# The gate rows of a first-layer expert as a stream of their own, and gathers counted as landing later

## The chip, the cores and the metric

The kernel runs on one core of one Trainium2 chip. The metric is the device time of one execution in microseconds. TensorE (PE) multiplies and transposes, ScalarE (ACT), VectorE (DVE) and GpSimd (POOL) work element by element, SyncE (SP) issues the weight loads, and POOL also issues the indirect transfers (gathers and scatters of rows).

## The reference

What is computed, cut to its core: sparse attention with a linear distance bias, then a mixture-of-experts layer whose tokens pick an expert, then one whose experts take at most 384 tokens each in the order of the sorted gate logits.

```python
x = attention(q, k, v, n_global, n_local)          # 4*768 = 3072 tokens, 512 features
# layer 1: tokens with x @ w_skip > 0 only
e_idx = argmax(xc @ w_gate);  gate_w = softmax(xc @ w_gate)[e_idx]
for e in range(8):
    h = maximum(xc[mask] @ w1[e], 0);  y[mask] = gate_w[mask, None] * (h @ w2[e])
out[do_compute] = xc + y
# layer 2: cap = 3072 // 8 = 384
order = argsort(-(x @ w_gate).flatten())
for idx in order:                                  # greedy, until all are assigned
    tok, e = idx // 8, idx % 8
    if assigned[tok] < 0 and counts[e] < cap: assigned[tok] = e; counts[e] += 1
for e in range(8):
    out[mask] = maximum(x[mask] @ w1[e], 0) @ w2[e]
```

## The kernel before

Attention runs until about 227 us. Layer 1 follows until about 494 us: `run_units` walks over eight experts' units, each of up to 256 tokens (two blocks of 128) and eight slices `f` of the hidden width. A unit's tokens are gathered by number from `xd` (tile xg), transposed through the one PSUM bank pt into xh (high part) and xl (low part), and multiplied with the split weights wh and wl: twelve 256-column matmuls into ph a slice, then, one slice late (`finish`), six 512-column ones into py. ACT makes hh from ph, DVE makes hl. A weight chunk wr is split by `W_.pump`: ACT writes wh, then DVE or POOL writes wl.

Six units are plain. Then one "extra" unit `X_` takes the tokens that overflowed; its tokens' tile is xgx. The last two units hold their second products back (`defer`), and these run beside the routing of layer 2. Layer 2 (about 516 to 835 us) has eight units of 384 tokens, with one routing phase of the next expert between the matmuls of each.

When a unit's py is complete, `epi1` calls `rows2`: the output rows o0 and o1 are made on DVE and scattered to `x2d`. Layer 2's gate logits of these rows, called gate rows here, need five more steps: o0 is transposed through pt into x2t, o1 too, x2t is multiplied with wg into pr (8 small matmuls), ACT copies that to ls, two transposes follow, and DVE sums lgo, which POOL scatters to `l2d`. Before the change these steps are tasks, one popped at the end of each slice, whatever is ready then. `last_rows` is a routing task of a slice of unit 1: POOL numbers a tile (iota into a tile that shares its buffer with x2t), and DVE computes from it.

The order in which work of different streams stands between the matmuls is decided when the program is built. A clock `ck` estimates each engine's time; after each matmul `hook` lets the stream of the lowest rank go on whose inputs are estimated ready (`Stream.when`), and `wait_for` steps streams until a condition holds. For a gather the clock counts 2.7 us plus `ck.late` until it has landed.

```python
    def when(self):
        eng, aps = self.need
        if eng == "pt":
            return ck.ready("pe", last_pt, aps) + (T_LOW if lows else 0)
    ...
        end += 2.7 + (self.late if over else 0)
```

Of the kernel before, what the change touches and what calls it, by code (L numbers as in the profile page):

```python
# [161 lines left out]
def tile_attn_moe_moe(ctx: ExitStack, tc: tile.TileContext, q, k, v, n_global, n_local,  # L162
# [366 lines left out]
    ck.late = T_G  # L529
# [326 lines left out]
    class Unit:  # L856
        at, tb, py, defer, xh = None, 0, 0, None, None
# [280 lines left out]
    class Stream:  # L1138
# [12 lines left out]
        def when(self):  # L1151
            eng, aps = self.need
            if eng == "pt":
                return ck.ready("pe", last_pt, aps) + (T_LOW if lows else 0)
            t = ck.ready(eng, (), aps)
            return max(t, ck.at["dve"] - T_SP) if eng == "dve" else t
# [42 lines left out]
    RANK = {"x": X_B, "ids": 0.5, "main": 2, "extra": 4}  # L1199

    def start(kind, gen):
        s_ = Stream(gen)
        s_.kind = kind
        s_.rank = lambda: RANK[kind] if len(result) <= unit_no[0] + T_L else {"x": 0, "main": 1, "ids": 2, "extra": 4}[kind]
        streams.append(s_)
# [7 lines left out]
    def run_units(units, nb, epilogue, tasks=(), between=None):  # L1213
# [13 lines left out]
        for s in range(len(units) * FC):  # L1227
# [21 lines left out]
            if u + 1 < len(units):  # L1249
                V_ = units[u + 1]  # L1250
                if V_.at is None and (V_.is_ready() or f == FC - 1):
                    V_.ready()
                    if V_.at is None:
                        V_.load()
            W_.pump()
            W_.pump()
# [23 lines left out]
    def epi1(U_, tasks):  # L1280
        nb = len(U_.xs)
        if U_.defer is not None:
            if U_.defer == 0:
                tasks.append(lambda: gate2(U_))
# [4 lines left out]
            return  # L1289
        rows2(U_)  # L1290
        U_.x2t = fx_.tile([128, KC, 256], F32, name="x2t")

        def tr(tb):
# [4 lines left out]
            nc.scalar.activation(U_.x2t[:, :, tb * 128:(tb + 1) * 128], p, AF.Copy)  # L1298

        def lg():  # L1300
            p = fps.tile([128, 256], F32, name="pr")
            n = nb * 128
            for c in range(KC):
                nc.tensor.matmul(p[c * 32:(c + 1) * 32, :n], wg2[:, c, :], U_.x2t[:, c, :n], start=True, stop=True)
            U_.ls = fx_.tile([128, 256], F32, name="ls1")
            nc.scalar.activation(U_.ls[:, :n], p[:, :n], AF.Copy)

        def lt():
            p = fps.tile([128, HI, KC, 32], F32, name="pr")
            for tb in range(nb):  # L1310
                nc.tensor.transpose(p[:, tb].rearrange("p c e -> p (c e)"), U_.ls[:, tb * 128:(tb + 1) * 128], ident)
            lgo = ff.tile([128, HI, E], F32, name="lgo")
            nc.vector.tensor_reduce(lgo[:, :nb], p[:, :nb, :, :E].rearrange("p j c e -> p j e c"),
                                    axis=AX.X, op=OP.add)
            for tb in range(nb):
                scatter(l2d, U_.sid[:, tb:tb + 1], lgo[:, tb], l2_st)
            U_.tasks = None

        U_.tasks = tasks
        for tb in range(nb):  # L1320
            tasks.append(lambda tb=tb: tr(tb))
        tasks.append(lg)
        tasks.append(lt)
        if U_ is not X_:
            tasks.extend(rt_tasks[:3])
            del rt_tasks[:3]
# [73 lines left out]
    def last_rows(tb):  # L1400
        d = fx_.tile([128, 2, 128], F32, name="x2t")
# [79 lines left out]
    def extra_rest(hs_):  # L1481
# [23 lines left out]
        while units1[NE - 1].tasks:  # L1505
            units1[NE - 1].tasks.pop(0)()
        tasks = []
        epi1(X_, tasks)
        for ap, t in zip((X_.x2[0], X_.x2t, None), tasks):
            yield "pe", [ap if ap is not None else X_.ls]  # L1510
            t()

    def between(U_, finish):
        if U_.defer == 1:
            wait_for(lambda: not [s_ for s_ in streams if s_.kind == "extra"])
            fxx.close()
# [3 lines left out]
        return extra(U_, finish)  # L1520
# [271 lines left out]
    split_next()  # L1792
    units2[0].load()
    split_next()
# [40 lines left out]
```

## Time and profile before

| | |
|---|---|
| median of 3 runs | 835.23 us (834.9 to 835.77) |
| the profiled execution | 842.16 us, of which the span from first to last instruction is 840.2 us |
| mean granted TensorE clock | 0.958 of full speed |
| busy: PE | 767.8 us, 91% of the span |
| busy: DVE, POOL, ACT | 524.5 (62%), 423.3 (50%), 409.0 us (49%) |
| moved by DMA | 132.82 MB, 158 GB/s |

TensorE is busy for most of the span, and the other engines feed it. So one looks for the places where it is idle or slow. The profile gives times in microseconds from the span's start. A matmul's row shows its start, its length and, in brackets, the idle time of TensorE just before it with what ended it.

### The profile page before, as it was taken

To read this page: it belongs to the slowest core of one execution; us is meant where nothing else is said; L and a number is where in the kernel's file an instruction comes from. 1 tells how busy PE (TensorE), PEld (TensorE's weight loads), DVE (VectorE), ACT (ScalarE), POOL (GpSimd) and SP (SyncE) were. 2 spreads that over 40 slices of the span, in tenths; PEclk is the share of its full clock that TensorE was granted. 3 is DMA by queue.
4 is the path that set the end of the run, shared out by engine and by line. 5 is a ranking of instruction groups with operands and counts; after the bars stand their busy time and mean duration, and the time that the engine had idled before them with its cause. 6 is when DMAs were issued, how large, how long until landed. Compare 5 with 4: busy or idle time off the path is not lost.

```text
span 840.2 us, 16697 instructions
## 1 busy us (share of the span) xinstructions
PE 767.8 (91%) x5711; PEld 635.7 (76%) x5711; DVE 524.5 (62%) x1896; ACT 409.0 (49%) x923; POOL 423.3 (50%) x569
## 2 busy tenths in 40 slices
PE   7999998998889999998979957999999999899994
PEld 5887777776578777887768735788888888799993
DVE  6988979886556565554353576677787777822110
ACT  5887887875455455544452222343342534335311
POOL 4654566743224444533360524694765938568501
PEclk9999999999969999999999985999999999999997
DMA  7787898878146566356560043336263643555100
GB/s 178 185 207 190 227 226 230 229 203 234 45 150 215 184 218 231 135 178 204 166 230 6 17 135 125 132 115 195 99 225 113 190 142 135 177 175 169 39 31 37
DMA packets 141013, 132.82 MB, mean 158 GB/s; under 512 B 62523, under 2 KB 107835, under 8 KB 140928
## 3 DMA queue, kind: packets, MB, share of 16 engines
q1 hardware_dynamic: 132160, 111.09, 44.4%
q0 software_dynamic: 7168, 20.26, 7.0%
q8 instruction: 46, 0.75, 0.4%
q10 hardware_dynamic: 1600, 0.39, 0.2%
q14 instruction: 39, 0.32, 0.1%
HBM read 109.55 MB, written 23.49 MB: 158 GB/s over the span
## 4 chain that ended last, share of the span: by engine, by line
PE 33%; issue 19%; POOL 11%; DVE 3%; DMA 3%; ACT 1%; POOLq 0%; SPq 0%; DVEq 0%
PE ph L123 14%; PE py L123 14%; POOL wl L123 6%; PE pr L123 3%; PE pt L123 2%; POOL out_dram L123 2%; DMA wr<-in_moe_w_dram 2%; DMA xg<-xd,gid 1%; POOL xg L123 1%; DVE bank L123 1%; ACT wh L123 1%; POOL x2d L123 1%; POOL l2d L123 1%; DVE wl L123 0%; DVE gm L123 0%
## 5 line engine op out<-in xcount | busy, mean ns | idle before, releaser
L123 POOL TENSOR_TENSOR wl<-wr,wh 128x1024 fp32r<-128x1024 f32 (+1 forms) x97 | 205.0, 2133 | 114.4 <-ACT wh L123 113.9
L123 ACT ACTIVATE hh<-ph 128x384 fp32r<-128x384 f32 (+2 forms) x130 | 56.7, 436 | 214.4 <-PE ph L123 206.9
L123 ACT ACTIVATE wh<-wr 128x1024 fp32r<-128x1024 f32 (+1 forms) x148 | 140.7, 984 | 40.4 <-PE py L123 22.9
L123 DVE SCALAR_TENSOR_TENSOR hl<-ph,hh 128x256 fp32r<-128x256 f32 (+1 forms) x128 | 62.3, 487 | 123.7 <-ACT hh L123 114.5
L123 PE MATMUL py<-wh,hl 128*128 128x512 f32 x320 | 128.7, 402 | 2.1 <-DVE hl L123 2.1
L123 PE MATMUL py<-wh,hh 128*128 128x512 f32 x320 | 128.8, 403 | 0.0
L123 PE MATMUL py<-wl,hh 128*128 128x512 f32 x320 | 128.4, 401 | 0.0
L123 POOL TENSOR_SCALAR pb<-pb,st 128x232 f32<-128x232 f32 (+1 forms) x192 | 83.6, 454 | 72.7 <-ACT pb L123 26.9
L123 ACT ACTIVATE pb<-sb,st 128x232 f32<-128x232 f32 (+1 forms) x192 | 114.0, 664 | 10.2 <-DVE st L123 9.7
L123 PE MATMUL ph<-xh,wh 128*128 128x256 f32 (+1 forms) x512 | 106.4, 326 | 3.2 <-ACT wh L123 1.5
L123 PE MATMUL ph<-xh,wl 128*128 128x256 f32 (+1 forms) x512 | 104.4, 322 | 0.0
L123 PE MATMUL ph<-xl,wh 128*128 128x256 f32 (+1 forms) x512 | 103.0, 321 | 0.9 <-DVE xl L123 0.9
L123 PEld LDWEIGHTS ph<-xh,wh 128*128 128x128 f32 x512 | 84.7, 195 | 12.9 <-ACT wh L123 2.0
L123 PEld LDWEIGHTS ph<-xl,wh 128*128 128x128 f32 x512 | 82.9, 196 | 1.2 <-DVE xl L123 1.1
L123 PEld LDWEIGHTS ph<-xh,wl 128*128 128x128 f32 x512 | 83.2, 196 | 0.4 <-issue 0.2
L123 DVE TENSOR_TENSOR wl<-wr,wh 128x1024 fp32r<-128x1024 f32 x51 | 65.1, 1301 | 24.4 <-ACT wh L123 24.1
L123 PEld LDWEIGHTS py<-wh,hl 128*128 128x128 f32 x320 | 60.4, 189 | 14.9 <-DVE hl L123 3.2
L123 DVE CUSTOM_DVE_ANT_0 sb<-pS,bias 128x232 f32<-128x232 f32 (+1 forms) x192 | 61.5, 374 | 8.6 <-PE pS L123 7.0
L123 PEld LDWEIGHTS py<-wl,hh 128*128 128x128 f32 x320 | 60.6, 189 | 7.9 <-issue 0.3
L123 PEld LDWEIGHTS py<-wh,hh 128*128 128x128 f32 x320 | 60.9, 190 | 7.3
L123 DVE COPY pts<-pP 116x512 f32<-116x512 f32 (+1 forms) x96 | 60.7, 672 | 7.5 <-PE pP L123 7.1
L123 PE MATMUL pS<-kt,qt 64*128 64x232 f32 (+1 forms) x384 | 50.7, 382 | 1.0 <-ACT pb L123 1.0
(448 smaller groups left out, 1200.2 us busy)
## 6 DMA issues: line engine op xcount, KB each, us to landing
wr<-in_moe_w_dram SPq DMA_DIRECT2D x136, 512.0 KB
xd<-xs SPq DMA_DIRECT2D x32, 192.0 KB
x2d<-xs SPq DMA_DIRECT2D x32, 192.0 KB
kraw<-in_k_dram SPq DMA_DIRECT2D x30, 192.0 KB
qraw<-in_q_dram SPq DMA_DIRECT2D x30, 192.0 KB
vw<-in_v_dram SPq DMA_DIRECT2D x32, 160.0 KB
vw<-in_v_dram SPq DMA_DIRECT2D x32, 120.0 KB
xT<-in_moe_w_dram SPq DMA_DIRECT2D x1, 1536.0 KB
```

The lines of the kernel that those rows point to most:

```text
L123: r = f(*a, **k)
```

## The change

The gate rows become a generator `gate_rows`, started by `epi1` as a stream of the new kind "turn", with ranks between those of the others. `epi1` of the next unit and `last_rows` first wait until no such stream is left. The extra unit runs its own gate rows inside its stream, and no longer pops unit 5's tasks. `ck.late` goes from 1 to 2.0, except around the gathers of layer 2's first unit, where it is 0. A step that needs pt waits for `T_LOW` after DVE's estimated time, no longer after the rows' own. The second `W_.pump()` of a slice is left out in six plain units when the first did a split and one of the two chunks would be split by an engine other than POOL. The 16 gate products of unit 6 (`gate2`) move from a task of unit 7 to the point where unit 6 has finished, ahead of the last wait for the extra stream.

```diff
@@ -526,7 +526,7 @@
     WWT, WWN = 1, (2, 5)
     T_GAP, T_SP, T_EPS, T_W, T_P, T_L, T_F, X_B, T_H, T_M, LEAN, T_G, DIRECT, CUT = 0, 0.65, 0.1, 0, 8, 1, 0.3, 3, -4, 0, 2, 1, 13, 16
     T_LOW = 0.7
-    ck.late = T_G
+    ck.late = 2.0
     W_ = Weights()
 
     class Pacer:
@@ -854,7 +854,7 @@
     slot_rest = slot_ids(gid, sid, gwt, psl, tmp1)
 
     class Unit:
-        at, tb, py, defer, xh = None, 0, 0, None, None
+        at, tb, py, defer, xh, x2 = None, 0, 0, None, None, None
 
     def x_load(U_, nb):
         U_.xs, U_.xt, U_.at, U_.tb = [], {}, ck.at["pe"], 0
@@ -1151,7 +1151,8 @@
         def when(self):
             eng, aps = self.need
             if eng == "pt":
-                return ck.ready("pe", last_pt, aps) + (T_LOW if lows else 0)
+                t = ck.ready("pe", last_pt, aps)
+                return max(t, ck.at["dve"] + T_LOW) if lows else t
             t = ck.ready(eng, (), aps)
             return max(t, ck.at["dve"] - T_SP) if eng == "dve" else t
 
@@ -1196,12 +1197,12 @@
             flush()
             U_.tb += 1
 
-    RANK = {"x": X_B, "ids": 0.5, "main": 2, "extra": 4}
+    RANK = {"x": X_B, "turn": 3.5, "ids": 0.5, "main": 2, "extra": 4}
 
     def start(kind, gen):
         s_ = Stream(gen)
         s_.kind = kind
-        s_.rank = lambda: RANK[kind] if len(result) <= unit_no[0] + T_L else {"x": 0, "main": 1, "ids": 2, "extra": 4}[kind]
+        s_.rank = lambda: RANK[kind] if len(result) <= unit_no[0] + T_L else {"x": 0, "turn": 0.5, "main": 1, "ids": 2, "extra": 4}[kind]
         streams.append(s_)
 
     def split2(U_):
@@ -1252,8 +1253,11 @@
                     V_.ready()
                     if V_.at is None:
                         V_.load()
+            n = W_.split
             W_.pump()
-            W_.pump()
+            if (W_.split == n or W_.split == len(W_.order) or u >= NE or not W_.helped(W_.order[n])
+                    or not W_.helped(W_.order[W_.split])):
+                W_.pump()
             if tasks:
                 tasks.pop(0)()
         finish()
@@ -1281,49 +1285,46 @@
         nb = len(U_.xs)
         if U_.defer is not None:
             if U_.defer == 0:
-                tasks.append(lambda: gate2(U_))
                 tasks.append(lambda: gate2_rows(U_))
                 tasks.append(table)
                 tasks.extend([lambda: None] * 3)
                 tasks.append(table_clear)
             return
+        wait_for(turned)
         rows2(U_)
-        U_.x2t = fx_.tile([128, KC, 256], F32, name="x2t")
-
-        def tr(tb):
+        if U_ is not X_:
+            start("turn", gate_rows(U_, nb))
+            tasks.extend(rt_tasks[:3])
+            del rt_tasks[:3]
+
+    def turned():
+        return not [s_ for s_ in streams if s_.kind == "turn"]
+
+    def gate_rows(U_, nb):
+
+        n = nb * 128
+        x2t = fx_.tile([128, KC, 256], F32, name="x2t")
+        for tb in range(nb):
+            yield "pt", [U_.x2[tb]]
             flush()
             p = turns()
             for c in range(KC):
                 nc.tensor.transpose(p[:, c], U_.x2[tb][:, c * 128:(c + 1) * 128], ident)
-            nc.scalar.activation(U_.x2t[:, :, tb * 128:(tb + 1) * 128], p, AF.Copy)
-
...
-        U_.tasks = tasks
+            nc.scalar.activation(x2t[:, :, tb * 128:(tb + 1) * 128], p, AF.Copy)
+        yield "pe", [x2t[:, :, :n]]
+        p = fps.tile([128, 256], F32, name="pr")
+        for c in range(KC):
+            nc.tensor.matmul(p[c * 32:(c + 1) * 32, :n], wg2[:, c, :], x2t[:, c, :n], start=True, stop=True)
+        ls = fx_.tile([128, 256], F32, name="ls1")
+        nc.scalar.activation(ls[:, :n], p[:, :n], AF.Copy)
+        yield "pe", [ls[:, :n]]
+        p = fps.tile([128, HI, KC, 32], F32, name="pr")
         for tb in range(nb):
-            tasks.append(lambda tb=tb: tr(tb))
-        tasks.append(lg)
-        tasks.append(lt)
-        if U_ is not X_:
-            tasks.extend(rt_tasks[:3])
-            del rt_tasks[:3]
+            nc.tensor.transpose(p[:, tb].rearrange("p c e -> p (c e)"), ls[:, tb * 128:(tb + 1) * 128], ident)
+        lgo = ff.tile([128, HI, E], F32, name="lgo")
+        nc.vector.tensor_reduce(lgo[:, :nb], p[:, :nb, :, :E].rearrange("p j c e -> p j e c"), axis=AX.X, op=OP.add)
+        for tb in range(nb):
+            scatter(l2d, U_.sid[:, tb:tb + 1], lgo[:, tb], l2_st)
 
     BITS = ((27, 32), (22, 32), (17, 32), (12, 32), (7, 32), (2, 32), (0, 4))
     NH = CAP // 128
@@ -1398,6 +1399,7 @@
     keep = rt.tile([128, NT], F32, name="keep")
 
     def last_rows(tb):
+        wait_for(turned)
         d = fx_.tile([128, 2, 128], F32, name="x2t")
         tk = rt.tile([128, 2], F32, name="tk")
         nc.gpsimd.iota(d[:, 0], pattern=[[NT, 128]], base=0, channel_multiplier=0, allow_small_or_imprecise_dtypes=True)
@@ -1502,22 +1504,20 @@
                                  start=c == 0 and i == 0, stop=c == FC - 1 and i == 2)
             W_.free = 4 * NE + (c + 1) // 2
             W_.pump()
-        while units1[NE - 1].tasks:
-            units1[NE - 1].tasks.pop(0)()
-        tasks = []
-        epi1(X_, tasks)
-        for ap, t in zip((X_.x2[0], X_.x2t, None), tasks):
-            yield "pe", [ap if ap is not None else X_.ls]
-            t()
+        epi1(X_, [])
+        yield from gate_rows(X_, 1)
 
     def between(U_, finish):
         if U_.defer == 1:
+            finish()
+            wait_for(lambda: X_.x2 is not None)
+            gate2(units1[NE])
             wait_for(lambda: not [s_ for s_ in streams if s_.kind == "extra"])
             fxx.close()
         if U_.defer is not None:
             pool = f1x.enter_context(tc.tile_pool(name=f"h{U_.defer}", bufs=1)) if U_.defer else hp7
             U_.h = [pool.tile([128, FC, SLOTS], F32R, name=f"{n}{U_.defer}", bufs=1) for n in ("hh", "hl")]
-        return extra(U_, finish)
+        return extra(U_, finish) or U_.defer == 1
 
     for tb in range(HI):
         x_turn(units1[0], tb, f"py{tb}")
@@ -1790,7 +1790,9 @@
         need(W_.order[W_.split])
 
     split_next()
+    ck.late = 0
     units2[0].load()
+    ck.late = 2.0
     split_next()
     split_next()
     wait_for(lambda: units2[0].tb == NH)
```

Three places in TensorE's order, as the program lists it. The first is the end of unit 0, where unit 1 begins: o_4755 and o_4761 are unit 0's two output blocks, py_4804 and py_4805 unit 1's sums. Before:

```order
L123 MATMUL pt<-ident,o_4755 128x128 x4
L123 MATMUL ph<-xh,wh 128x256 x4
L123 MATMUL ph<-xl,wh 128x256 x4
L123 MATMUL ph<-xh,wl 128x256 x4
L123 MATMUL py_4804<-wh,hh 128x512
L123 MATMUL py_4804<-wl,hh 128x512
L123 MATMUL py_4804<-wh,hl 128x512
L123 MATMUL py_4805<-wh,hh 128x512
L123 MATMUL py_4805<-wl,hh 128x512
L123 MATMUL py_4805<-wh,hl 128x512
L123 MATMUL pt<-ident,o_4761 128x128 x4
```

After:

```order
L123 MATMUL py_4520<-wh,hl 128x512
L123 MATMUL pt<-ident,o_4755 128x128 x4
L123 MATMUL pt<-ident,o_4761 128x128 x4
L123 MATMUL pr<-x2t,wg_79 32x256 x4
L123 MATMUL pr<-ident,ls_4793 128x128 x2
L123 MATMUL ph<-xh,wh 128x256 x4
L123 MATMUL ph<-xl,wh 128x256 x4
```

The two transposes and the two gate products, formerly each a slice apart, now follow one another, ahead of unit 1's second slice.

The second place is the end of unit 4, with the extra unit's tokens xgx; o_6004 and o_6010 are unit 4's output blocks. Before:

```order
L123 MATMUL py_6053<-wh,hl 128x512
L123 MATMUL py_6054<-wh,hh 128x512
L123 MATMUL py_6054<-wl,hh 128x512
L123 MATMUL pt<-ident,xgx 128x128 x4
L123 MATMUL py_6054<-wh,hl 128x512
L123 MATMUL pt<-ident,o_6010 128x128 x4
L123 MATMUL ph<-xh,wh 128x256 x4
L123 MATMUL ph<-xl,wh 128x256 x4
```

After, from the block o_6010 on (o_6004 stands five rows earlier):

```order
L123 MATMUL pt<-ident,o_6010 128x128 x4
L123 MATMUL py_6041<-wh,hl 128x512
L123 MATMUL ph<-xh,wh 128x256 x4
L123 MATMUL ph<-xl,wh 128x256 x2
L123 MATMUL pr<-x2t,wg_79 32x256 x4
L123 MATMUL pt<-ident,xgx 128x128 x4
L123 MATMUL ph<-xl,wh 128x256 x2
L123 MATMUL pr<-ident,ls_6080 128x128 x2
```

The transpose of xgx has moved from ahead of o_6010 to behind the product of x2t.

The third place is the last routing phase in layer 2, beside its seventh unit: tb_rhs and mp are what DVE makes for the phase, xg_10482 the first gathered block for the last unit. Before, from the phase's first product on:

```order
L123 LDWEIGHTS tri
L123 MATMUL pt<-ttb,tri 128x1
L123 MATMUL py_10495<-wh,hh 128x512
L123 MATMUL py_10495<-wl,hh 128x512
L123 MATMUL py_10495<-wh,hl 128x512
L123 MATMUL py_10496<-wh,hh 128x512
L123 MATMUL py_10496<-wl,hh 128x512
L123 MATMUL py_10496<-wh,hl 128x512
L123 MATMUL ph<-xh,wh 128x384 x4
L123 MATMUL pt<-ident,xg_10482 128x128 x4
L123 MATMUL ph<-xl,wh 128x384 x4
```

After:

```order
L123 LDWEIGHTS tri
L123 MATMUL pt<-ttb,tri 128x1
L123 MATMUL py_10500<-wh,hh 128x512
L123 MATMUL py_10500<-wl,hh 128x512
L123 MATMUL py_10500<-wh,hl 128x512
L123 MATMUL py_10501<-wh,hh 128x512
L123 MATMUL py_10501<-wl,hh 128x512
L123 MATMUL py_10501<-wh,hl 128x512
L123 MATMUL py_10502<-wh,hh 128x512
L123 LDWEIGHTS mp
L123 MATMUL pt<-tb_rhs,mp 128x27
L123 LDWEIGHTS mp
```

The products of tb_rhs and mp now stand ahead of the first gathered block, which comes sixteen rows later after that first product than it did.

## Rows read from the trace of the kernel before

**Rows 1.** Stretches: length, busy us of PE PEld DVE ACT POOL, PEclk, DMA, GB/s.

```profile
282.00:384.00 102.00, 93.36 (x614) 80.75 (x612) 56.12 (x108) 49.87 (x77) 45.11 (x55) 1.00 0.53 179
411.00:444.00 33.00, 26.71 (x169) 23.09 (x168) 17.15 (x23) 17.75 (x29) 16.54 (x15) 0.90 0.65 220
516.00:726.00 210.00, 209.45 (x1325) 171.59 (x1326) 161.21 (x696) 82.24 (x119) 134.65 (x87) 0.97 0.45 146
```

**Rows 2.** Stretches of 3 to 4 us, same columns.

```profile
380.00:384.00 4.00, 0.81 (x6) 0.49 (x4) 1.91 (x3) 2.49 (x3) 2.58 (x3) 1.00 0.87 318
384.10:387.50 3.40, 3.40 (x17) 3.40 (x17) 0.00 (x0) 0.60 (x1) 1.55 (x2) 0.50 0.99 302
438.70:442.10 3.40, 3.33 (x16) 3.33 (x17) 1.02 (x2) 0.98 (x2) 0.80 (x2) 0.50 0.40 146
```

**Rows 3.** Timeline, VectorE, then TensorE, 254 to 258 us: start, length, what [idle before].

```profile
254.10 3.18 DVE L123 TENSOR_TENSOR wl<-wr,wh 128x1024 fp32r<-128x1024 f32 x2 [0.80 <-ACT wh L123]
257.67 0.50 PE L123 MATMUL py<-wh,hl 128*128 128x512 f32 x1 [1.15 <-DVE hl L123]
```

**Rows 4.** Timeline of TensorE, 423 to 428 us.

```profile
424.55 0.65 PE L123 MATMUL pt<-ident,o 128*128 128x128 f32 x4 [0.69 <-ACT x2t L123]
425.89 0.64 PE L123 MATMUL pr<-x2t,wg 128*32 128x256 f32 x8 [0.69 <-ACT x2t L123]
427.04 0.44 PE L123 MATMUL pr<-ident,ls 128*128 128x128 f32 x2 [0.51 <-ACT ls L123]
```

**Rows 5.** Timeline, 287 to 296 us: VectorE, GpSimd, TensorE.

```profile
292.62 0.29 DVE L123 TENSOR_SCALAR x2t<-x2t,tk 128x128 f32<-128x128 f32 x1 [4.26 <-POOL spacer L123]
289.99 2.41 POOL L123 TENSOR_TENSOR wl<-wr,wh 128x1024 fp32r<-128x1024 f32 x1 [6.39 <-ACT wh L123]
294.49 0.50 PE L123 MATMUL py<-wh,hl 128*128 128x512 f32 x1 [0.98 <-DVE hl L123]
```

**Rows 6.** Timeline of TensorE, places between 274 and 360 us.

```profile
276.66 0.63 PE L123 MATMUL pt<-ident,xg 128*128 128x128 f32 x4 [0.80 <-DMA xg<-xd,gid]
304.95 0.63 PE L123 MATMUL pt<-ident,xg 128*128 128x128 f32 x4 [1.20 <-DMA xg<-xd,gid]
322.04 0.39 PE L123 MATMUL py<-wl,hh 128*128 128x512 f32 x1
322.27 0.39 PE L123 MATMUL py<-wh,hl 128*128 128x512 f32 x1
322.86 0.66 PE L123 MATMUL pt<-ident,o 128*128 128x128 f32 x4 [0.21 <-DVE o L123]
359.12 0.63 PE L123 MATMUL pt<-ident,xg 128*128 128x128 f32 x4 [1.13 <-DMA xg<-xd,gid]
```

**Rows 7.** Timeline, 377 to 386 us: VectorE, then TensorE.

```profile
382.18 1.23 DVE L123 TENSOR_TENSOR wl<-wr,wh 128x1024 fp32r<-128x1024 f32 x1 [2.09 <-ACT wh L123]
383.32 0.68 DVE L123 TENSOR_TENSOR tl<-pt,th 128x512 fp32r<-128x512 f32 x1
384.06 1.12 PE L123 MATMUL pt<-ident,o 128*128 128x128 f32 x4 [3.26 <-DVE tl L123]
```

**Rows 8.** Timeline, 426 to 447 us: TensorE, then GpSimd.

```profile
438.77 1.11 PE L123 MATMUL pt<-ident,xg 128*128 128x128 f32 x4 [2.48 <-DMA xg<-xd,gid]
446.10 0.73 PE L123 MATMUL ph<-xl,wh 128*128 128x256 f32 x4 [0.94 <-DVE xl L123]
432.71 1.03 POOL L123 DMA_INDIRECT xg<-xd,gid  x1 [0.30 <-issue]
```

**Rows 9.** Timeline, 492 to 517 us: GpSimd.

```profile
503.98 0.99 POOL L123 DMA_INDIRECT xg<-x2d,ids  x1 [4.91 <-DVE bank L123]
```

**Rows 10.** Tile ma: its eight writers; timelines of GpSimd, TensorE, 726 to 738 us.

```profile
L123 DVE TENSOR_SCALAR ma<-islot,fx x8: 408/412/4407, 496.7 to 729.8; 128x384 f32<-128x384 f32 x8
729.27 4.71 POOL L123 TENSOR_TENSOR wl<-wr,wh 128x1024 fp32r<-128x1024 f32 x2
734.33 0.66 PE L123 MATMUL pt<-ident,xg 128*128 128x128 f32 x4 [2.91 <-DVE tb_rhs L123]
```

More of the change, by code (lines that the diff above doesn't have):

```diff
@@ L1297, in tr @@
                 nc.tensor.transpose(p[:, c], U_.x2[tb][:, c * 128:(c + 1) * 128], ident)
-            nc.scalar.activation(U_.x2t[:, :, tb * 128:(tb + 1) * 128], p, AF.Copy)
[L1300 to L1317, printed above, removed]
-        U_.tasks = tasks
-        for tb in range(nb):
-            tasks.append(lambda tb=tb: tr(tb))
-        tasks.append(lg)
-        tasks.append(lt)
-        if U_ is not X_:
-            tasks.extend(rt_tasks[:3])
-            del rt_tasks[:3]
+            nc.scalar.activation(x2t[:, :, tb * 128:(tb + 1) * 128], p, AF.Copy)
[7 more added lines that the diff above has]
+        p = fps.tile([128, HI, KC, 32], F32, name="pr")
+        for tb in range(nb):
+            nc.tensor.transpose(p[:, tb].rearrange("p c e -> p (c e)"), ls[:, tb * 128:(tb + 1) * 128], ident)
[3 more added lines that the diff above has]
+            scatter(l2d, U_.sid[:, tb:tb + 1], lgo[:, tb], l2_st)
     BITS = ((27, 32), (22, 32), (17, 32), (12, 32), (7, 32), (2, 32), (0, 4))
```

## The prediction

> **What bounds the kernel now.** I read the stretches first. In layer 2 TensorE is busy for 209.45 of 210 us; in layer 1 for 93.36 of 102 us and then for 26.71 of 33 us [rows 1]. The reader is to see that layer 2 leaves nothing but its last phase to win, while layer 1 loses 8.6 and 6.3 us to single waits; the timelines show those. A wait on TensorE adds its length to the run, since TensorE has no spare time to give back. I count each wait at its idle time plus 0.15 us: a 512-column matmul that runs on starts 0.23 us after the one ahead (322.04, 322.27), and the transposes of an output block that waited 0.21 us start 0.59 us after it, 0.36 us too late [rows 6].
>
> A long wait has a second price. From 380 to 384 us TensorE worked 0.81 of 4 us, and from 384.1 to 387.5 us its granted clock was 0.50, thus 1.2 GHz for 2.4; after the wait that ended at 438.77 us the same follows, 3.40 us long [rows 2, 8]. At half speed 3.40 us do the work of 1.7 us, so 1.7 us are lost each time.
>
> **The change part by part.** No arithmetic is added or taken away. What moves is when each step stands in its engine's queue, so the sum is one of waits.
>
> *End of unit 0.* Two wl splits of DVE, 3.18 us together, stand ahead of an hl, and TensorE waits 1.15 us for it [rows 3]. With one split at a time the hl comes behind the first: -1.3 us.
>
> *Unit 0 to unit 1.* The first task of unit 1 is `last_rows`, which now waits until unit 0's gate rows are done, and so forces all of them at once, with no matmul between. The price of such a heap is in the trace: at the end of unit 5 the three waits of the same four steps were 0.69, 0.69 and 0.51 us [rows 4], with restarts +2.35. Now for POOL: the l2d scatters stand ahead of the iota, for which `last_rows` holds DVE; the hl behind it comes late, priced by the wait of 1.15 us above: +1.3. At the second `last_rows` DVE stood 4.26 us behind an iota that was queued behind a 2.41 us split on POOL, and TensorE waited 0.98 us [rows 5]; this order dissolves: -1.13. The gather's wait of 0.80 us [rows 6] goes, as its transpose stands a slice later: -0.95. Two stalls close together may drop the clock, as the 3 to 4 us waits of [rows 2] did; I take half of 1.7: +0.85. The place gives +2.4. Bounds: nothing for the held DVE and no drop, +0.3; a hold as long as the 4.26 us, less the 1.4 us that six matmuls cover (6 x 0.23), and a full drop, +4.9.
>
> *Units 1 to 4.* Three gathers are waited for at three boundaries; the first and the last of them cost 1.20 and 1.13 us [rows 6], with restarts 1.35 and 1.28, together about 4. Their transposes now stand one to one and a half microseconds later. I leave 0.3 to 0.5 us at each, 1.1 in all: -2.9. Four waits for an output block (0.36 each) go, since the transposes now stand behind matmuls: -1.45. Together -4.35; if the gathers themselves are issued later by as much, only -1.45.
>
> *The extra unit's tokens.* xgx was transposed into the one pt bank, so the next block's transpose had to wait for tl on DVE, which stood behind a wl of 1.23 us and that behind ACT: 3.26 us [rows 7], and the clock dropped. Now o1 comes ahead of xgx, and the next user of pt is far behind: -3.4 - 1.7 + 0.2 for a short wait of the next gather = -4.9.
>
> *Unit 5, the extra unit, unit 6.* The heap of [rows 4] goes, as these steps are woven between matmuls: -2.35. Unit 7's gathers are issued ahead of the scatters, and the first transpose stands between the extra unit's products; the wait of 2.48 us and its clock drop go: -2.65 - 1.7. With the transposes spread, the 0.94 us wait for xl goes too [rows 8]: -1.1. Against it: unit 5's steps between the extra unit's matmuls may wait as an output block does, three times 0.36, +1.1; unit 6 still pumps two splits a slice, and one hl may be late as in [rows 3], +1.3; the extra unit's own gate rows, formerly between ph matmuls, form a heap behind unit 6's gate products, +2.35, with half a clock drop, +0.85. Net -2.2; bounds -7.8 (all hidden) and +2.15 (the gather's wait and its drop stay).
>
> *The routing's end.* The gathers for layer 2 are issued only at 503.98 us, POOL having been idle for 4.91 us until the routing's result [rows 9]. That chain is not shortened; `gate2` costs the same 16 products wherever it stands. 0, at most 0.6 either way.
>
> *Layer 2.* Here the clock's later gathers reorder every phase. Where TensorE already waits for nothing, there is nothing to win. The exception is the last phase: ma takes 0.41 us in the median, but 4.41 us when it meets POOL's two wl (4.71 us from 729.27), and TensorE waits 2.91 us [rows 10]. The products of mp now stand ahead of the gather's transpose, so the wait comes earlier by some four matmuls and gets longer by about 1.1 us less what the moved transposes give back: +0.5. If ma gets ahead of POOL, 2.91 + 0.15 and a drop of 1.7 go: -4.8.
>
> A rule of the Trainium skill bears on ma. The row shows it held from 729.80 to 734.2 us, across both splits. The page "SBUF — State Buffer", section "Who interferes with whom", says that VectorE and GpSimd share a port pair, that a tensor_scalar can take it, and that whoever issues first holds it for one whole instruction. By that ma would run after the first split, some 2.4 us sooner, and the last phase would cost 2.4 us less; the row says that the second split got in first too, and the row goes into the sum.
>
> **The sum.** -1.3 + 2.4 - 4.35 - 4.9 - 2.2 + 0 + 0.5 = -9.85 us on the profiled 842.16 us, so 832.3. The runs shown have a median of 835.23, 6.9 us below that execution; the waits are the same kind in both, so I take the sum over whole: 825.4 us. A difference of 0.2%, 1.7 us, is about what a measurement of this kernel can tell from none.
>
> **The rivals.**
> 1. *ma gets ahead of POOL.* DVE has one hl instead of two between ids and ma, which speaks for it; but two operations on the table that stood ahead of ids now stand behind it. Then -9.85 - 0.5 - 4.8 = -15.1: 820.1 us.
> 2. *The waits move along.* A gather is issued when the earlier unit's state lets it, and a held DVE delays the next hl. If units 1 to 4 give only -1.45 and unit 6's place +2.15: -9.85 + 2.9 + 4.35 = -2.6, 832.6 us. For it speaks that 1.1 us of later place is little against waits of 1.2 us.
> 3. *Slower: ma meets POOL's pair in other phases too.* Eight phases have such an ma, one was caught [rows 10]. All phases are moved against POOL's splits. Each new catch costs some 4 us of wait and 1.7 of clock, 5.7. Two give +1.55 (836.8), three +7.25 (842.5); from the second on the gain is gone. Against it: the phases' splits come at most in pairs and seven of eight went clear.
> 4. *Nothing to measure.* Heaps at two places and later gathers eat what the others give: -1 to +1, within 834 to 837 us. Against it speaks the wait for tl alone, -4.9, whose cause plainly leaves the order.
>
> **The numbers.** My forecast 0.50 (its own range 821 to 830), rival 1 0.15, rival 2 0.15, rival 3 0.12 (a third of it with two catches, which is no measurable change), rival 4 0.08. Faster 0.50 + 0.15 + 0.15 = 0.80; same: rival 4 without a quarter, 0.06, and a third of rival 3, 0.04: 0.10; slower 0.10. The range leaves out rival 3 and 4 and the best end of rival 1: 817 to 834.
>
> **What would show it.** In the new trace: no wait for tl near 384 us and a full clock behind it; no gap behind three gathers; a heap of four steps at the end of unit 0 with gaps of 0.5 to 0.7 us, and another behind unit 6's gate products; a first gather for unit 7 without a 2.5 us wait; ma near 0.4 us in seven phases and about 4.4 us in one. It would be wrong if several ma run 4 us long, if the gather waits come back at other rows, or if the held DVE at unit 1 stops TensorE for more than 3 us.

## The result and the profile after

The changed kernel takes 823.88 us (median of 4 runs, 821.7 to 825.96) against 835.5 us (4 runs, 834.9 to 835.9): ratio 0.9853, 95% interval 0.9828 to 0.9879. That is 11.6 us less; 825.4 was forecast. On two chips of the experiments it was 824.09 against 836.51 us (e4_after: 0.9847, 0.9830 to 0.9865) and 825.04 against 836.51 us (e9_after: 0.9860, 0.9840 to 0.9881). For e4_after two theories stood on record: 14 to 17 us under before (the change gives little beyond the later count of the gathers, which alone had given 14.3 us) and 10 to 13 us (as at first). It came to 12.4, the second.

The profiled execution of the changed kernel is the fastest of the four; its span is 819.9 us, its mean granted clock 0.966. These are the stretches that answer to [rows 1]; the columns are the same, and the borders have moved with the program:

```profile
282.00:376.00 94.00, 92.56 (x626) 81.63 (x624) 55.75 (x88) 47.47 (x75) 44.95 (x48) 1.00 0.63 199
402.00:435.00 33.00, 28.15 (x209) 24.18 (x209) 18.66 (x27) 18.24 (x30) 14.71 (x15) 1.00 0.62 209
501.00:711.00 210.00, 209.16 (x1328) 172.00 (x1328) 162.58 (x701) 83.55 (x120) 136.06 (x87) 0.98 0.45 147
```

In the units 1 to 4 TensorE is now idle for 1.4 of 94 us, where it was 8.6 of 102; around the extra unit for 4.9 of 33, where it was 6.3. The long stretch of layer 2 is as it was. The clock stood at full speed in both stretches of layer 1.

The end of unit 0 on TensorE (to set beside [rows 4]):

```profile
263.32 0.66 PE L123 MATMUL pt<-ident,o 128*128 128x128 f32 x4 [0.20 <-DVE o L123]
264.67 0.66 PE L123 MATMUL pt<-ident,o 128*128 128x128 f32 x4 [0.69 <-ACT x2t L123]
266.01 0.64 PE L123 MATMUL pr<-x2t,wg 128*32 128x256 f32 x8 [0.69 <-ACT x2t L123]
267.15 0.44 PE L123 MATMUL pr<-ident,ls 128*128 128x128 f32 x2 [0.50 <-ACT ls L123]
```

This is the heap that the prediction took over from the end of unit 5: gaps of 0.69, 0.69 and 0.50 us between four steps, within a hundredth of what they were there. What follows on GpSimd, VectorE and TensorE (beside [rows 5]):

```profile
268.80 1.01 POOL L123 DMA_INDIRECT l2d<-lgo,sid  x1 [0.23 <-issue]
270.11 0.99 POOL L123 DMA_INDIRECT l2d<-lgo,sid  x1 [0.22 <-issue]
271.10 0.28 POOL L123 IOTA x2t<- 128x128 f32 x1
271.41 0.58 DVE L123 TENSOR_SCALAR x2t<-x2t,tk 128x128 f32<-128x128 f32 x1 [3.49 <-POOL x2t L123]
273.56 0.50 PE L123 MATMUL py<-wh,hl 128*128 128x512 f32 x1 [0.81 <-DVE hl L123]
275.27 3.34 DVE L123 TENSOR_TENSOR wl<-wr,wh 128x1024 fp32r<-128x1024 f32 x1
280.65 0.50 PE L123 MATMUL py<-wh,hl 128*128 128x512 f32 x1 [1.18 <-DVE hl L123]
```

Two scatters to l2d stand ahead of the iota, VectorE stands 3.49 us idle until it is done, and TensorE then waits 0.81 us for the hl behind it. It waits 1.18 us for another hl behind the second `last_rows`; there VectorE was late for another reason: its own split, 1.22 us elsewhere, took 3.34 us beside one of GpSimd (2.40 us from 275.13).

The gathers of the units 2 to 4 (beside [rows 6]) and the place of xgx (beside [rows 7]), TensorE:

```profile
332.92 0.66 PE L123 MATMUL pt<-ident,xg 128*128 128x128 f32 x4 [0.29 <-DVE xl L123]
359.50 0.66 PE L123 MATMUL pt<-ident,xg 128*128 128x128 f32 x4 [1.15 <-DVE xl L123]
373.95 0.60 PE L123 MATMUL pt<-ident,o 128*128 128x128 f32 x4
376.00 0.66 PE L123 MATMUL pt<-ident,xgx 128*128 128x128 f32 x4
380.13 0.60 PE L123 MATMUL pt<-ident,xg 128*128 128x128 f32 x4
```

Of three waits for gathers of about 1.2 us none is left in this trace; waits of 0.29 and 1.15 us have come in their place, and these are for VectorE's xl of the block before, which still holds the bank pt. In the other two traces of the changed kernel the gather at the start of unit 2 is waited for again, 0.59 us (e4_after) and 1.09 us (e9_after). The transposes of o1, xgx and of unit 6's first block have no idle time ahead of them at all; the wait of 3.26 us is gone.

Unit 7's first gather and the end of unit 6 on TensorE (beside [rows 8]):

```profile
412.67 0.60 PE L123 MATMUL pt<-ident,xg 128*128 128x128 f32 x4
428.32 0.29 PE L123 MATMUL pr<-hl,ww 128*16 128x256 f32 x1 [0.98 <-DVE hl L123]
430.66 0.42 PE L123 MATMUL pr<-x2t,wg 128*32 128x128 f32 x8 [0.75 <-ACT x2t L123]
431.54 0.33 PE L123 MATMUL pr<-ident,ls 128*128 128x128 f32 x1 [0.46 <-ACT ls L123]
```

The gather is not waited for any more. The extra unit's own gate rows form the second heap, with an hl ahead of it (0.98, 0.75, 0.46 us). Ahead of these stand two more late hl in unit 6, 0.50 us at 418.26 and 0.90 us at 420.86.

The last routing phase (beside [rows 10]). First GpSimd's first gather before the change; then, after it, the row numbers `ids` of that gather on VectorE, GpSimd's rows, and the eight writers of ma:

```profile
725.74 0.98 POOL L123 DMA_INDIRECT xg<-x2d,ids  x1 [3.40 <-DVE ids L123]
```

```profile
708.38 0.16 DVE L123 SCALAR_TENSOR_TENSOR ids<-pt,ix 128x3 int32<-128x3 f32 x1
708.16 2.41 POOL L123 TENSOR_TENSOR wl<-wr,wh 128x1024 fp32r<-128x1024 f32 x1 [8.05 <-ACT wh L123]
710.76 0.98 POOL L123 DMA_INDIRECT out_dram<-o,ids  x1 [0.16 <-issue]
712.05 0.99 POOL L123 DMA_INDIRECT xg<-x2d,ids  x1 [0.30 <-DVE fe L123]
715.59 4.76 POOL L123 TENSOR_TENSOR wl<-wr,wh 128x1024 fp32r<-128x1024 f32 x2
L123 DVE TENSOR_SCALAR ma<-islot,fx x8: 408/411/466, 479.4 to 713.3; 128x384 f32<-128x384 f32 x8
```

ma takes 0.47 us at most, in all eight phases. GpSimd's order is another one than before. There it stood idle for 3.40 us until ids was made and issued the gather 0.43 us after ids began; the pair of splits behind the three gathers started at 729.27 us, 0.5 us ahead of ma. Now a single split and a scatter to the output stand ahead of the three gathers when ids comes, the first gather is issued 3.67 us after ids, and the pair starts at 715.59 us, 2.3 us after ma (713.26). The wait of 2.91 us and the clock drop behind it are gone.

### The profile page after: what moved, and what is told of

It reads as the page before. It is cut to its first block, busy times and chain, and to the rows that moved or that the text cites. A ratio compares the mean times of both kernels' runs of the same rounds, so it can differ in the third digit from the quotient of the medians.

```text
span 819.9 us, 16691 instructions
## 1 busy us (share of the span) xinstructions
PE 758.0 (92%) x5711; PEld 630.0 (77%) x5711; DVE 525.3 (64%) x1896; ACT 408.1 (50%) x923; POOL 426.9 (52%) x569
## 4 chain that ended last, share of the span: by engine, by line
PE 62%; DVE 13%; issue 11%; POOL 7%; ACT 4%; DMA 3%; another core or an unknown queue 0%; SPq 0%; POOLq 0%; DVEq 0%; ACTq 0%
PE ph L123 20%; PE py L123 19%; PE pP L123 9%; PE pS L123 4%; PE pO L123 4%; POOL wl L123 4%; PE pr L123 3%; PE pt L123 2%; DVE sb L123 2%; DVE pts L123 2%; DMA wr<-in_moe_w_dram 2%; DVE wl L123 2%; ACT wh L123 1%; POOL out_dram L123 1%; DVE bank L123 1%
## 5 line engine op out<-in xcount | busy, mean ns | idle before, releaser
L123 DVE TENSOR_TENSOR wl<-wr,wh 128x1024 fp32r<-128x1024 f32 x51 | 68.8, 1355 | 23.2 <-ACT wh L123 23.1
L123 PE MATMUL pP<-ident,pb 128*116 128x128 f32 (+1 forms) x384 | 51.2, 277 | 0.0
```

What stands on the lines that cost most here:

```text
L123: r = f(*a, **k)
```

## The experiments

All times are medians; each kernel was compared with the kernel before on its own chip. Going by their numbers, e0 to e3 ran on one chip, e4 to e7 on a second, e8 to e11 on a third. VectorE is called held when an operation of it stands still beside GpSimd's splits, or, at the start of unit 1, behind the iota; ma is "caught" when the pair of splits holds it.

**The kernel before once more (e0_before).** No edit.

> The kernel before, unchanged, profiled once more. Its first profiled execution took 842.16 us against a median of 835.5, that of the changed kernel 821.7 against 823.9. Theory A (the gain is the waits of layer 1, about 11.7 us; the end of attention, 3.4 us, and the last phase of layer 2, 4.8 us, were chance of that one execution): ma takes 0.4 to 0.5 us in all eight phases, TensorE does not wait for it, and the execution takes 834 to 837 us. Theory B (the caught ma belongs to the order before and the change frees it): ma takes 4.4 us in the last phase again, TensorE waits 2.9 us, and the execution takes 840 us or more.

Measured: 839.27 us, beside nine runs of the same kernel on this chip with a median of 841.05. The eight writers of ma:

```profile
L123 DVE TENSOR_SCALAR ma<-islot,fx x8: 410/414/4406, 494.0 to 727.0; 128x384 f32<-128x384 f32 x8
```

One is caught again, and the wait of 2.91 us ahead of the transposes at 731.49 us is there. So the catch belongs to the order before, as theory B has it. The time of this run decides nothing between the theories, since this chip is some 5 us slower for the same kernel. The start of layer 1 (the first ph) differs between executions without any edit there: 238.87 and 238.03 us in the two traces of before, 235.43 in the changed kernel, 235.62 in a kernel with before's order (e6_ma_accum).

**The later count alone (e1_only_late, and again as e8_only_late).** Edit to the kernel before:

```diff
-    ck.late = T_G
+    ck.late = 2.0
...
+    ck.late = 0
     units2[0].load()
+    ck.late = 2.0
```

> The kernel before with nothing but the gathers counted as landing 1 us later (and as landing at once for layer 2's first unit). Theory A: of layer 1's waits only those for gathers go, three of 1.2 us and the one of 2.5 us with its clock drop at most: 3 to 6 us faster than before, 829.5 to 832.5. Theory B: it is the new order of layer 2 that counts, so this alone gives 8 us or more: under 827.5. A third way: the transposes of the gathers are moved onto the output blocks in the one pt bank, and nothing is gained: 834 to 837.

> The kernel before with only the later count of gathers, once more, now on one chip with the changed kernel. Theory A' (the number alone gives what the whole change gives, since the heaps that the rest forms cost what it saves): within 2 us of the changed kernel. Rival (the two ratios, 0.9836 and 0.985, came from different chips and hide a difference): the changed kernel is faster by 2 us or more, as the sum of the prediction has it: -1.3 + 2.4 for the ends of units 0 and 1, -1.45 for the output blocks, -2.35 for the heap of unit 5.

> The changed kernel, as the measure for the other three on this chip: 822 to 826 us, 11 to 16 us under its before.

Measured first: 826.74 against 841.05 us, ratio 0.9836 (0.9822 to 0.9849), 14.3 us. Then, on one chip with the changed kernel: 823.89 us (0.9852, 0.9830 to 0.9874) beside 825.04 us of the changed kernel (0.9860, 0.9840 to 0.9881) and 836.51 us of before. So the count alone (2.0, and 0 for the gathers of layer 2's first unit) gives what the whole change gives, within the noise. How much of it the 0 has was not tried. The second trace, the writers of ma and then TensorE:

```profile
L123 DVE TENSOR_SCALAR ma<-islot,fx x8: 408/410/1330, 483.4 to 716.3; 128x384 f32<-128x384 f32 x8
379.91 0.63 PE L123 MATMUL pt<-ident,xg 128*128 128x128 f32 x4 [0.93 <-DMA xg<-xd,gid]
413.70 0.66 PE L123 MATMUL pt<-ident,o 128*128 128x128 f32 x4 [0.69 <-ACT x2t L123]
415.04 0.64 PE L123 MATMUL pr<-x2t,wg 128*32 128x256 f32 x8 [0.69 <-ACT x2t L123]
416.19 0.44 PE L123 MATMUL pr<-ident,ls 128*128 128x128 f32 x2 [0.51 <-ACT ls L123]
```

The wait for tl at xgx is gone here too: xgx is transposed at 375.14 us, and the next gather (379.91) is waited for 0.93 us instead of pt for 3.26. ma took 1.33 us at most, in the first phase, as it did before the change; in the last it is free. The heap of unit 5 is still there with its 0.69, 0.69 and 0.51 us; the changed kernel has taken it away and has two others.

**The change without the later count (e2_no_late).** Edit to the changed kernel: `ck.late` is 1 throughout, as before.

> The changed kernel with gathers counted as before. Theory A: three waits of about 1.2 us come back, with restarts some 3 us: 826 to 828. Theory B: layer 2 loses its new order, 5 us or more: 829 and up.

Measured: 834.27 us, ratio 0.9918 (0.9904 to 0.9931), 6.8 us under before. Both theories' numbers were for the first chip; against this chip's before it gives half of what the later count alone gave there. The writers of ma, and two waits of TensorE at transposes of gathered blocks:

```profile
L123 DVE TENSOR_SCALAR ma<-islot,fx x8: 407/410/4392, 490.2 to 725.0; 128x384 f32<-128x384 f32 x8
306.50 0.63 PE L123 MATMUL pt<-ident,xg 128*128 128x128 f32 x4 [1.75 <-DMA xg<-xd,gid]
336.18 0.93 PE L123 MATMUL pt<-ident,xg 128*128 128x128 f32 x4 [2.14 <-DVE xl L123]
```

These waits are longer than those before (1.20 and 1.34 us); the first is for the gather, the second for VectorE's xl and so for pt. ma is caught. The gain that is left is in layer 1, where xgx goes without its wait here as well.

**Which layer (e5_late_layer1).** Edit to the kernel before: `ck.late = 2.0`, and `ck.late = T_G` ahead of `units2[0].load()`.

> The kernel before with gathers counted 1 us later in layer 1 only; layer 2 counts as before. Theory A' (two places: layer 1's waits give 9 to 10 us, the caught ma of the last phase 4.8): 8 to 11 us under before, with ma at 4.4 us in the last phase and the wait of 2.9 us behind it. Rival (layer 2's order is disturbed by when layer 1 ends, and its ma comes free as well): 13 us or more under before.

Measured: 827.94 against 836.51 us, ratio 0.9895 (0.9876 to 0.9914): 8.6 us, as theory A' has it. TensorE in the last phase:

```profile
719.98 0.66 PE L123 MATMUL pt<-ident,xg 128*128 128x128 f32 x4 [2.91 <-DVE tb_rhs L123]
```

The wait of 2.91 us is there, and ma took 4.41 us. The changed kernel on this chip is 12.4 us under before (824.09). If the later count alone gives the same here as it did on the third chip (e8_only_late; it did not run on this one), layer 1 has some 8.6 of it and layer 2's order the other 3.8, an estimate.

**What holds ma (e6_ma_accum).** Edit to the kernel before; every engine's order stays the same:

```diff
-        dv.tensor_scalar(ma, islot, fx[:, 3:4], None, op0=OP.is_ge)
+        mac = rt.tile([128, 1], F32, name="mac")
+        dv.eng.tensor_scalar(ma, islot, fx[:, 3:4], 0.0, op0=OP.is_ge, op1=OP.add, accum_out=mac)
+        ck.done("dve", "tensor_scalar", [ma], [islot, fx[:, 3:4]], 1)
```

> The kernel before, in the same order, with ma written by a tensor_scalar that also adds up its result (an extra sum of 128 numbers that nobody reads). By the Trainium skill's page SBUF - State Buffer, section Who interferes with whom, this form does not take the port pair that VectorE shares with GpSimd. If that is what held ma: it takes 0.4 to 0.7 us in all phases beside GpSimd's two splits, the wait of 2.9 us and the clock drop behind it go, 4 to 5.5 us under before. If ma was held by something else (its data, or a form that is held as well): ma takes 4.4 us again and the time is that of before within 1.5 us.

Measured: 834.88 against 836.51 us, ratio 0.9978 (0.9963 to 0.9992), 1.6 us. VectorE, GpSimd and TensorE in the last phase:

```profile
724.94 0.60 DVE L1713 TENSOR_SCALAR_CACHE_REDUCE ma<-islot,fx 128x384 f32<-128x384 f32 x1
725.59 4.05 DVE L123 SCALAR_TENSOR_TENSOR mp<-islot,fx,ma 128x384 bf16<-128x384 f32 x1
724.46 4.76 POOL L123 TENSOR_TENSOR wl<-wr,wh 128x1024 fp32r<-128x1024 f32 x2
730.30 0.66 PE L123 MATMUL pt<-ident,xg 128*128 128x128 f32 x4 [1.41 <-DVE xl L123]
```

ma ran free beside the two splits: 0.60 us in all eight phases, 0.2 longer than its old form runs alone. But mp, the next operation, which takes 0.62 us elsewhere, now took 4.05 us, until the splits were done. TensorE waits 1.41 us for the xl behind mp instead of 2.91 for tb_rhs, and the clock keeps its level. So it was ma's form that let the splits hold it, as expected. The gain was expected at 4 to 5.5 us and came to 1.6 (0.7 to 3.1), since the hold passed to the next operation: 1.5 us of the wait went. The drop of 1.7 us that followed the wait in both traces of the kernel before went too; the two together, 3.2 us, lie at the upper edge of that interval. The page "SBUF — State Buffer" of the Trainium skill, section "Who interferes with whom", has the hold of mp too: a VectorE operation with two inputs in SBUF contends with a GpSimd operation that reads SBUF. It also says that the one that comes second waits until the first has finished. By that ma would have waited for one split; here ma and mp each waited for two (4.41 and 4.05 us beside 4.71 and 4.76), so the measurement decides: the pair held them like one operation.

**The first heap (e3_later_task).** Edit to the changed kernel:

```diff
+            if U_ is units1[0]:
+                tasks.extend([lambda: None] * 2)
             tasks.extend(rt_tasks[:3])
```

> The changed kernel with two empty tasks ahead of the first routing tasks, so that last_rows comes two slices later and unit 0's gate rows are woven between matmuls. Theory A (the heap of four steps costs what its gaps show, 0.85, 0.85 and 0.46 us from start to start, and the held DVE about 1.1): 2 to 3.3 us faster than the changed kernel, 820.5 to 822. Rival (last_rows holds DVE wherever it stands and the gaps come back at the hl): within 1 us of the changed kernel, 823 to 825.

Measured: 825.45 against 841.05 us, ratio 0.9811 (0.9791 to 0.9830). The bounds in microseconds were for the first chip; the changed kernel did not run on this one. The later count alone ran here and on the third chip, and over it e3_later_task is about 2.4 us faster than the changed kernel (826.74 less 825.45 here, 825.04 less 823.89 there). That is an estimate over four medians whose runs spread by 3 to 5 us; it speaks for theory A and does not show it. In the trace the heap's gaps are gone, VectorE stands idle for as long as before, and TensorE's wait for the hl behind that has grown. GpSimd, VectorE, TensorE:

```profile
275.67 2.43 POOL L123 TENSOR_TENSOR wl<-wr,wh 128x1024 fp32r<-128x1024 f32 x1
278.03 0.27 POOL L123 IOTA x2t<- 128x128 f32 x1
278.33 0.57 DVE L123 TENSOR_SCALAR x2t<-x2t,tk 128x128 f32<-128x128 f32 x1 [3.47 <-POOL x2t L123]
280.48 0.50 PE L123 MATMUL py<-wh,hl 128*128 128x512 f32 x1 [1.80 <-DVE hl L123]
```

A split of 2.43 us now stands ahead of the iota as well, and one wait of 1.80 us replaces those of 0.81 and 1.18; a new one of 0.71 us for ls stands at 379.59 us.

**Two splits a slice (e10_two_pumps).** Edit to the changed kernel: `W_.pump()` twice without a condition.

> The changed kernel with two weight splits a slice throughout, as before the change. Theory (one hl behind two wl of DVE at the end of unit 0 costs 1.1 to 1.3 us, the later units hide theirs): 1 to 2 us slower than the changed kernel. Rival (splits that come sooner let the first ph of the extra unit's second half start earlier, a wait of 1.6 us for wh): 0.5 us or more faster.

Measured: 829.59 us, ratio 0.9915 (0.9897 to 0.9932), 4.6 us slower than the changed kernel on this chip; 1 to 2 were expected, so the direction is the theory's and its price too small. ACT, and TensorE at two places:

```profile
385.41 1.06 ACT L123 ACTIVATE wh<-wr 128x1024 fp32r<-128x1024 f32 x1 [1.74 <-DMA wr<-in_moe_w_dram]
331.90 0.50 PE L123 MATMUL py<-wh,hl 128*128 128x512 f32 x1 [1.40 <-DVE hl L123]
386.79 0.44 PE L123 MATMUL pr<-ident,ls 128*128 128x128 f32 x2 [1.41 <-ACT ls L123]
```

The price is not at the end of unit 0 alone. An hl is 1.40 us late in a later unit; and ACT, which has the next wh ahead of ls in its queue, stands 1.74 us waiting for the weights' load, and TensorE waits 1.41 us for ls. Not all of the 4.6 us is traced to such waits. The rival is out: the wait of 1.46 us for wh in the extra unit is there in both kernels.

**Both heaps apart (e7_woven), and only the first (e11_own_row).** Edit of e11_own_row to the changed kernel:

```diff
-            if (W_.split == n or W_.split == len(W_.order) or u >= NE or not W_.helped(W_.order[n])
+            if (W_.split == n or W_.split == len(W_.order) or u > NE or not W_.helped(W_.order[n])
...
+    row0 = fx_.tile([128, 128], F32, name="row0")
+    nc.gpsimd.iota(row0, pattern=[[NT, 128]], base=0, channel_multiplier=0, allow_small_or_imprecise_dtypes=True)
+
     def last_rows(tb):
-        wait_for(turned)
-        d = fx_.tile([128, 2, 128], F32, name="x2t")
+        d = fx_.tile([128, 2, 128], F32, name="lr")
         tk = rt.tile([128, 2], F32, name="tk")
-        nc.gpsimd.iota(d[:, 0], pattern=[[NT, 128]], base=0, channel_multiplier=0, allow_small_or_imprecise_dtypes=True)
...
-        nc.vector.tensor_scalar(d[:, 0], d[:, 0], tk[:, 0:1], None, op0=OP.subtract)
+        nc.vector.tensor_scalar(d[:, 0], row0, tk[:, 0:1], None, op0=OP.subtract)
```

e7_woven has the same and one line more:

```diff
-                return max(t, ck.at["dve"] + T_LOW) if lows else t
+                return (t + T_LOW if self.kind == "extra" else max(t, ck.at["dve"] + T_LOW)) if lows else t
```

> The changed kernel with the two heaps taken apart: last_rows reads a row of numbers written once, ahead of layer 1, into a buffer of its own, and waits for no gate rows; the extra unit's gate rows count DVE's time as before the change and so stand between unit 6's matmuls; unit 6 pumps one split at a time. If the gaps seen in the changed kernel are the price (heaps 2.2 and 2.3 us, hl behind the held DVE 1.1 and 1.4, hl behind two splits 0.7, 1.1 and 0.8): 5 to 9 us faster than the changed kernel on this chip. Rival (the waits come back at other rows, or splits that come one at a time are late for unit 7): within 2 us of it.

> The changed kernel with last_rows reading its own row of numbers and with one split at a time in unit 6, the extra unit's gate rows left where the change has them. Theory (the heap and the held DVE at unit 0 cost 2.2 + 1.1 + 1.4, the split behind unit 6's hl 0.7 + 1.1): 4 to 6 us faster than the changed kernel. Rival (as with the two heaps taken apart, which gave 2.3 us of an expected 5 to 9): 1 to 3 us faster, the rest coming back behind unit 6.

Measured: e7_woven 821.83 us beside 824.09 of the changed kernel (ratios 0.9812, 0.9793 to 0.9831, and 0.9847), 2.3 us faster, nearer to its rival than to the 5 to 9 of its theory. TensorE, and VectorE ahead of the later wait:

```profile
417.83 0.63 PE L123 MATMUL pt<-ident,o 128*128 128x128 f32 x4 [1.88 <-DVE xl L123]
428.30 0.74 PE L123 MATMUL ph<-xh,wh 128*128 128x256 f32 x4 [1.56 <-DVE hl L123]
425.51 2.40 DVE L123 TENSOR_TENSOR wl<-wr,wh 128x1024 fp32r<-128x1024 f32 x1 [0.51 <-ACT wh L123]
```

The gate rows stand between matmuls as meant, but their first transpose comes while pt still holds a gathered block whose xl VectorE has not made: 1.88 us. And TensorE waits 1.56 us for a later hl, which stands behind a split of VectorE that took 2.40 us beside one of GpSimd.

e11_own_row leaves those gate rows where the change put them: 819.02 us, ratio 0.9780 (0.9762 to 0.9799), beside 825.04 us on the same chip. That is 6.0 us faster than the changed kernel, and of the two theories' 4 to 6 and 1 to 3 the first. TensorE's waits at unit 0 and around unit 6:

```profile
273.79 0.50 PE L123 MATMUL py<-wh,hl 128*128 128x512 f32 x1 [0.68 <-DVE hl L123]
423.10 0.74 PE L123 MATMUL ph<-xh,wh 128*128 128x256 f32 x4 [1.08 <-DVE hl L123]
427.53 0.43 PE L123 MATMUL pr<-x2t,wg 128*32 128x128 f32 x8 [0.46 <-ACT ma L123]
428.41 0.33 PE L123 MATMUL pr<-ident,ls 128*128 128x128 f32 x1 [0.46 <-ACT ls L123]
```

At unit 0 one wait of 0.68 us is left of the heap and the two late hl. Half of the second heap went too: its first transpose now stands at 424.15 us, ahead of the gate products, with no idle time before it. The run has two edits at once, last_rows and the splits of unit 6, and they weren't tried apart. Layer 1 is 4.4 us shorter than in the changed kernel's trace on this chip; the rest of the 6.0 us isn't traced.

## Why the prediction was right, and where not

The forecast, 825.4 us, lies 1.5 us from the result. Its steps in layer 1 hold, the one on layer 2 doesn't. That the number came so near is in part luck, since the two errors that this left have opposite signs: the sum is too small, mostly by the last phase (5.3 us), and it was read from an execution 6.9 us longer than the median that it was taken off. Rival 1, which has the last phase right, gives 820.1 us, 3.8 us too low. From the two profiled executions, by the measure of the prediction (idle time plus 0.15 us):

| step | forecast | measured |
|---|---|---|
| end of unit 0 | -1.3 | -1.3, the wait is gone |
| unit 0 to unit 1 | +2.4 | +2.5: heap 2.3, two hl 2.3, less the waits of 0.95 and 1.13; no clock drop |
| units 1 to 4 | -4.35 | -3.5: gathers -2.4, three of the four output blocks -1.1 (the fourth still waits 0.20 us, at 263.32) |
| the extra unit's tokens | -4.9 | -5.1, with the clock drop |
| unit 5, extra unit, unit 6 | -2.2 | -3.1: waits 6.6, now 5.2 (without the 1.46 for wh in both); the drop behind the gather -1.7 |
| a clock drop at 414.5 us before, which this execution does not have | 0 | -1.7 |
| the routing's end | 0 | +0.8 (from the last py to layer 2's first ph 22.4 us, now 23.2; the cause is open) |
| the last phase | +0.5 | -4.8 |

**The step that failed is the last phase.** The prediction put ma behind GpSimd's pair of splits at the same place as before; in place of +0.5 it measured -4.8. What ran there is its first rival, but not by the rival's reason (one hl less on VectorE between ids and ma): with one hl less VectorE still took 4.88 us from ids to ma, and 4.49 before. It is GpSimd that came later, with its first gather 3.67 us after ids in place of 0.43, behind a split and a scatter, and so the pair starts after ma. That it is the later count which does this is shown: ma is caught in the traces of e0_before, e2_no_late and e5_late_layer1, which count layer 2's gathers as before, and took 1.33 us at most in all nine with the later count. One argument that the prediction had against more catches is misread: GpSimd's splits come in runs of up to five (11.82 us from 660.91 in the trace before), and not seven but six of the eight ma went clear, the first taking 1.33 us beside another operation of GpSimd.

**The terms do not say which line of the change earns them.** The prediction gave the streams the wait at xgx and the waits around unit 6. The later count alone takes most of the first too (3.26 us, now 0.93) and a part of the second (the gather's 2.48 us, now 1.50; the heap of unit 5 stays), and no clock drop follows either wait in its two traces (e8_only_late, e1_only_late). The streams without the count give half of its gain (e2_no_late). Put together they give no more than the count alone, because the change pays for the heap of unit 5 with two new ones and with the held VectorE; e11_own_row, which takes away the first, the held VectorE and half of the second, gains 6.0 us where their gaps gave 6.5. In unit 6 the prediction had one late hl (1.3); three came (2.8 with restarts, 0.5 before). The single split is needed with the streams (e10_two_pumps, 4.6 us); the count alone reaches its time without it. The new wait for pt (`T_LOW`) and the move of `gate2` weren't tried alone.

**The sum was too small and its base too long.** The measured terms add up to -16.2 us, the medians differ by 11.5 to 12.4. The execution profiled before took 842.16 us, 6.7 more than the median of the runs beside it, and the one after 821.7, 2.2 less than its median. Of the 20.3 us between their spans 3.4 lie ahead of layer 1, where nothing was edited (first ph at 238.87 and 235.43 us); the other 16.9 are near the sum of the terms. So the pair shows more than an average pair would.

In the traces with before's order layer 1 (first ph to last py) took 254.5, 252.7 and 253.2 us, in those of the changed kernel 242.1, 246.3 and 242.8: -9.8 in the mean. The first three have three clock drops each in it (after the low clock at its start), the others none, three and one, so that about 2.8 of the 9.8 us are drops. Layer 2 (first ph to the end) took 324.4 and 324.1 us against 319.2, 319.2 and 320.2: -4.7. The routing between takes 0.6 more. That is -13.9 us, and about 2 us between traces and medians stay open, as does what makes one chip 5 us slower than the others for the kernel before. The changed kernel did not run on that chip; the later count alone was 2.9 us slower there than on the third (826.74 and 823.89 us).

## What to carry to other kernels

When a planner sets the order, compare its estimates with the trace first. Here a gather was counted as landed 3.7 us after the end of its issue, and in layer 1 before the change the five transposes that waited for one ran 4.9 to 5.4 us after it. Counting 1 us more gave as much by itself as the whole change, in layer 1 by waits that went and in layer 2 by an order in which a table's operation no longer meets a pair of splits; that second part was not foreseen. A barrier in the program ("wait until these steps are done") turns steps that were hidden between matmuls into a heap, and the heap can be priced before it is built, from the same steps standing bare elsewhere in the trace. Then take away what the barrier protects, here a shared buffer and an iota issued late (e11_own_row), and do not only move the barrier: that took the heap away and left the late hl (e3_later_task, 1.80 us).

## What the runs showed of the hardware

An operation of VectorE was held by two splits of GpSimd in a row as if they were one (4.41 us beside 4.71, in four traces), and when its form was changed so that it ran free (0.60 us), the next one with two inputs was held in its place (4.05 us). VectorE's own split, 1.22 us alone, took 3.34 us in the changed kernel beside a single split of GpSimd (2.40 us).

The clock drops come and go between executions of one kernel. The first trace of the changed kernel has none in layer 1 after 242 us. The second, on another chip, has these stretches (columns as in [rows 2]):

```profile
405.20:408.40 3.20, 3.20 (x20) 2.17 (x18) 0.00 (x0) 0.98 (x2) 2.74 (x3) 0.50 0.77 219
432.50:439.10 6.60, 6.04 (x33) 5.32 (x34) 1.08 (x5) 0.72 (x3) 1.84 (x3) 0.50 0.00 0
```

The first begins after the wait for wh, which all traces have (1.45 or 1.46 us) and which such a drop follows in six of the fourteen; the second, of two pieces in a row, at the heap behind unit 6. Each 3.4 us at 1.2 GHz costs 1.7 us against 2.4 GHz, so three of them move an execution by 5 us, which is more than most edits here.
